# The first tile's last twelve products in both arms of a branch, and a row of conversions moved among the last expert's further tiles

## The chip, the cores and the metric

The kernel runs on one core of one Trainium2 chip. A time is the time of one execution in microseconds (us) as the device measures it; of several runs the median is given. The profile is of one execution, which has its own time.

## The reference

Sliding-window attention with a few sink positions is followed by a mixture of eight experts, and that by a gated layer (GLU). Of these the middle one matters here:

```python
expert_idx = np.argmax(x @ w_gate, axis=1)            # 1536 tokens, 8 experts
# token i takes the next free row of its expert, up to capacity = 384 rows
h = np.maximum(np.einsum('ecd,edf->ecf', disp, w1), 0.0)   # d = 512, f = 1024
y = np.einsum('ecf,efd->ecd', h, w2)
out[i] = gate_w[i] * y[expert_idx[i], pos[i]]
# GLU: sigmoid(x @ w_gate) * (x @ w_val) @ w_out, 1536 x 512 -> 1536 -> 512
```

How many tokens an expert gets is known only while the kernel runs.

## The kernel before, in words

All products are done at about fp32's precision: an operand is split into a high part (rounded to the matmul's type) and a low part (the rest), and a product is taken as high x high, low x high and high x low. `products` therefore lists twelve matmuls for a 128 x 512 x 512 product: four with the high activations and the high weights, four with the low activations, four with the low weights. ScalarE (ACT) makes a high part by a cast, VectorE (DVE) the low part by a subtraction that needs the cast's result.

`experts` runs over the experts e = 0 to 7. Each expert has up to three tiles of 128 rows. The first tile is computed always, the second and third under `If` on the expert's count (`more_tiles`, L837 and L839). In this run's data experts 0 and 7 have three tiles, 3 and 5 have two, and 1, 2, 4 and 6 have one. A tile goes through these steps:

- `turn_x` (L730 to L734): TensorE (PE) turns the rows, ACT casts `xh`, DVE subtracts `xl`.
- two times twelve products with the two halves of w1 into `u`, each followed by a relu on ACT (L763, `hr`); `turn_h` (L769 to L773) turns its result into `hh` and `hl`. The turns stand six products late, so that PE has work while ACT does the relu.
- twelve products with each half of w2; the second twelve need the second `hh` and `hl`. Then ACT copies the result to `yr` (L778), and `put_y` turns it (L787) and puts it into `yh` and `yl`, the input of the GLU (L789, L790).

For the first tile of an expert `put_y` stands in the next expert, behind twelve products. For the second and third tiles nothing stands between a tile's steps but what is shown here: a second tile starts with `turn_x` behind the branch.

All engines work off their own instructions in program order. Beside the tiles, ACT and DVE split the weights of the next expert (`split_next`, L132 and L133: 1024 columns each), ten halves ahead; the last three of an expert's splits stand ahead of the branch. The GLU's weights come as 64-bit floats and are converted: `whole` turns 512 columns by one ACT step (L150) and three DVE steps (L151, L153, L157), `convert` splits them (L164 on ACT, L165 on DVE). In the last expert `whole(0)` and `convert(0)` stand ahead of the branch, and seven further calls are the list `fills`; `beside()` in a tile takes the next one, and the arms for fewer tiles do what is left (`rest`).

PE, ACT and DVE each take the branch by themselves; an arm that is not taken is jumped over.

Of the kernel before, what the change touches and what calls it, by code (L numbers as in the profile page):

```python
# [9 lines left out]
F32 = mybir.dt.float32  # L10
# [10 lines left out]
P = 128  # L21
SUB = 1024
# [4 lines left out]
def kernel(  # L27
# [16 lines left out]
    nc = tc.nc  # L44
# [8 lines left out]
    N = B * S  # L53
# [644 lines left out]
    def experts(yh, yl):  # L698
        with ExitStack() as st:
# [27 lines left out]
            def turn_x(raw, more):  # L727
                t = ps_t.tile([P, KD, P], F32, tag="t", name="t")
                for k in range(KD):
                    nc.tensor.transpose(t[:, k], raw[:, k * P:(k + 1) * P], ident)  # L730
                h_ = ht.tile([P, KD, P], F32R, tag=f"xh{more}", name="xh")
                l_ = ht.tile([P, KD, P], F32R, tag=f"xl{more}", name="xl")
                nc.scalar.copy(out=h_, in_=t)  # L733
                nc.vector.tensor_sub(out=l_, in0=t, in1=h_.bitcast(F32))  # L734
                return h_, l_
# [7 lines left out]
            def weights(n):  # L743
                t = pair[n % NDBL].rearrange("p w (b k f) -> p w k b f", b=2, k=4)
                return t[:, 0], t[:, 1]
# [27 lines left out]
                nc.vector.tensor_sub(out=l_, in0=t, in1=h_.bitcast(F32))  # L773
                return h_, l_

            def raw_y(ps, more):
                t = hp.tile([P, 512], F32, tag=f"yr{more}", name="yr", bufs=1)
                nc.scalar.copy(out=t, in_=ps)  # L778
                return t

# [16 lines left out]
                nc.vector.tensor_copy(out=yh[:, d], in_=z)  # L797
                nc.gpsimd.tensor_copy(out=yl[:, d], in_=z)

            def more_tiles(e, fills):  # L800

                w1a, w1b, w2a, w2b = (weights(4 * e + x) for x in range(4))

                def one(j, todo):
                    def beside():
                        for f in todo[:1]:
                            f()
                        del todo[:1]

                    x = turn_x(xe[:, j - 1], 1)  # L810
                    u = bank(ps_u, 1)
                    go(products(u, x, w1a, True, True))
                    beside()
                    ra = relu(u)
                    u = bank(ps_u, 1)
                    b = products(u, x, w1b, True, True)
                    go(b[:6])
                    ha = turn_h(ra, 0)
                    beside()
                    go(b[6:])  # L820
                    rb = relu(u)
                    beside()
                    y = bank(ps_y, 1)
                    a = products(y, ha, w2a, True, False)
                    go(a[:6])
                    hb = turn_h(rb, 1)
                    beside()
                    go(a[6:])
                    go(products(y, hb, w2b, False, True))
                    return raw_y(y, 1)  # L830

                def rest(todo):
                    for f in todo:
                        f()

                n = 4 * (len(fills) + 1) // 8
                with tc.If(cnt_e[e] > P) as more:  # L837
                    put_y(e, 1, one(1, fills[:n]))
                    with tc.If(cnt_e[e] > 2 * P) as most:  # L839
                        put_y(e, 2, one(2, fills[n:]))  # L840
                    if fills:
                        with most.Else():
                            rest(fills[n:])
                if fills:
                    with more.Else():
                        rest(fills)

            V = nc.vector
            xs = {0: load_x(0), 1: load_x(1)}
# [5 lines left out]
            for e in range(E):  # L855
                w1a, w1b, w2a, w2b = (weights(4 * e + j) for j in range(4))
                m = 8 * e
                if e:
                    load_x_next(e + 2)
                    load_more(e)  # L860
                    split_next(m + 2, V)
                    split_next(m + 3, V)
                u = bank(ps_u, 0)
                go(products(u, x, w1a, True, True))
                ra = relu(u)
                if e:
                    put_y(e - 1, 0, yr)
                    split_next(m + 4, V)
                else:
                    cnt_x = counts([nc.sync.engine])  # L870
                    for j in range(1, E):
                        nc.sync.dma_start(
                            out=slots[j * ROWS:(j + 1) * ROWS, :][bass.ds(cnt_x[j], P), :], in_=zero)
                    load_more(e)
                    load_x_next(2)
                u = bank(ps_u, 0)
                b = products(u, x, w1b, True, True)
                go(b[:6])
                ha = turn_h(ra, 0)
                if e:  # L880
                    split_next(m + 5, V)
                go(b[6:])
                rb = relu(u)
                if e:
                    split_next(m + 6, V)
                if e + 1 < E:
                    x = turn_x(xs[e + 1], 0)
                y = bank(ps_y, 0)
                a = products(y, ha, w2a, True, False)
                go(a[:6])  # L890
                hb = turn_h(rb, 1)
                if e:
                    split_next(m + 7, V)
                go(a[6:])
                if e:
                    split_next(m + 8, V)
                    split_next(m + 9, V)
                elif e == 0:
                    cnt_e = counts([nc.tensor.engine, nc.scalar.engine, nc.vector.engine])
                go(products(y, hb, w2b, False, True))  # L900
                yr = raw_y(y, 0)
                if e == 0:
                    pi = order(hp)
                elif e < 7:
                    order_ids(pi, 2 * (e - 1), 2 * e)
                fills = []
                if e + 1 == E:
                    whole(0, 0, SUB)
                    convert(0)
                    load_glu(4, 0)  # L910
                    for q in range(1, 4):
                        fills += [partial(whole, q, h * 512, h * 512 + 512) for h in range(2)]
                        if q == 1:
                            fills.append(partial(convert, 1))
                more_tiles(e, fills)
            load_glu(5, 1)
            load_ids()
            put_y(E - 1, 0, yr)

            kept = nc.values_load(  # L920
                cnt_i[0:1, 2 * E:], engines=[nc.scalar.engine, nc.vector.engine], min_val=0, max_val=N,
                skip_runtime_bounds_check_because="a count of the tokens")
            z = zeros.unsqueeze(1).to_broadcast([P, KD, P])
            nc.scalar.copy(out=yh[:, :, bass.ds(kept, P)], in_=z)
            nc.vector.tensor_copy(out=yl[:, :, bass.ds(kept, P)], in_=z)
            for q in range(2, 4):
                convert(q)
                load_glu(q + 4, q)
# [270 lines left out]
```

## Time and profile before

| | us |
|---|---|
| median of 3 runs (lowest and highest) | 661.77 (659.67 to 663.36) |
| the profiled execution: its time | 662.41 |
| its span, first to last instruction | 660.7 |
| PE busy in the span | 613.9 |
| DVE, ACT busy | 359.7, 306.1 |
| experts, first product to the GLU's first | 147.61 to 363.26 |

The span is what the rows below are measured in; the time is 1.71 us longer. PE's clock has two levels, 2.4 GHz (granted clock 1.00) and 1.2 GHz (0.50); its mean over the span is 0.964.

### The profile page before, as it was taken

The numbers are of one execution on the slowest core, as the hardware profiler recorded it, in microseconds if no ns is written. First come the engines' busy times: TensorE is split into PE (matmuls) and PEld (weight loads), VectorE is DVE, ScalarE is ACT, GpSimd is POOL, SyncE is SP. The second block draws the span as 40 slices with busy tenths as digits, with TensorE's granted clock in tenths as the row PEclk, the third lists the DMA queues.
The fourth block names the chain that finished last, engine by engine and source line by source line (L and its number), as shares of the span: only waits on it lengthen the run. The fifth ranks groups of instructions, "written<-read, shape, count | busy, mean of one in ns | idle before, by whom it ended". The sixth has DMA issues, their size and how long they took to land.

```text
span 660.7 us, 9362 instructions
## 1 busy us (share of the span) xinstructions
PE 613.9 (93%) x3323; PEld 507.5 (77%) x3323; DVE 359.7 (54%) x871; ACT 306.1 (46%) x590; POOL 109.2 (17%) x163
## 2 busy tenths in 40 slices
PE   9899989989799899989697999999999997999995
PEld 5888888947577677767575888888888886889993
DVE  3465556534128655828754999981238811128911
ACT  4567757512238656838643655551225411125411
POOL 3155868472400000000000000000200000200002
PEclk9899969989999899999899899999999999799999
DMA  8987967142009963937712555551102520102101
GB/s 195 289 240 241 320 166 228 50 148 96 0 1 303 319 208 101 340 102 229 255 60 64 191 191 191 191 191 64 63 1 81 189 113 4 59 9 73 55 1 68
DMA packets 43638, 94.07 MB, mean 142 GB/s; under 512 B 5664, under 2 KB 24352, under 8 KB 39728
## 3 DMA queue, kind: packets, MB, share of 16 engines
q1 hardware_dynamic: 39872, 86.24, 40.5%
q0 software_dynamic: 2304, 6.09, 2.5%
q10 hardware_dynamic: 1392, 0.86, 0.5%
q8 instruction: 38, 0.62, 0.4%
q14 instruction: 32, 0.26, 0.1%
HBM read 82.63 MB, written 10.75 MB: 141 GB/s over the span
## 4 chain that ended last, share of the span: by engine, by line
issue 27%; PE 21%; ACT 2%; POOL 1%; DVE 1%; POOLq 0%; DVEq 0%; ACTq 0%
PE u L759 4%; PE g L168 4%; PE g L170 4%; PE g L169 4%; PE acc L170 2%; PE acc L168 2%; PE acc L169 2%; POOL out_dram L1024 1%; PE t L769 0%; DVE stage L153 0%; ACT pair L132 0%; ACT yr L778 0%; ACT hh L772 0%; PE t L787 0%; DVE stage L157 0%
## 5 line engine op out<-in xcount | busy, mean ns | idle before, releaser
L168 PE MATMUL g<-yh,pair 128*128 128x512 f32 (+1 forms) x288 | 110.4, 383 | 7.7 <-issue 4.6
L169 PE MATMUL g<-yl,pair 128*128 128x512 f32 (+1 forms) x288 | 110.0, 382 | 0.0
L170 PE MATMUL g<-yh,pair 128*128 128x512 f32 (+1 forms) x288 | 109.9, 382 | 0.0
L1024 POOL DMA_INDIRECT out_dram<-o,ids x11 | 10.8, 980 | 468.4 <-ACT o L1040 465.9
L759 PE MATMUL u<-pair,xh 128*128 128x512 f32 x224 | 64.4, 416 | 12.4 <-ACT xh L733 9.0
L992 DVE TENSOR_TENSOR g<-g,g 128x512 f32<-128x512 f32 (+1 forms) x36 | 23.4, 651 | 91.4 <-PE g L170 89.4
L993 ACT CAST gh<-g 128x512 fp32r<-128x512 f32 (+1 forms) x36 | 21.4, 594 | 110.6 <-DVE g L992 106.6
L133 DVE TENSOR_TENSOR pair<-stage,pair 128x1024 fp32r<-128x1024 f32 x54 | 64.2, 1220 | 11.7 <-ACT pair L132 11.3
L168 PEld LDWEIGHTS g<-yh,pair 128*128 128x128 f32 x288 | 55.2, 192 | 17.0 <-issue 5.0
L132 ACT CAST pair<-stage 128x1024 fp32r<-128x1024 f32 x64 | 65.3, 1050 | 3.0 <-PEq L837 1.5
L759 PE MATMUL u<-pair,hh 128*128 128x512 f32 x224 | 61.5, 400 | 2.7 <-ACT pair L132 1.8
L169 PEld LDWEIGHTS g<-yl,pair 128*128 128x128 f32 x288 | 55.3, 192 | 8.3
L759 PEld LDWEIGHTS u<-pair,xh 128*128 128x128 f32 x224 | 42.5, 197 | 24.6 <-ACT xh L733 10.6
L170 PEld LDWEIGHTS g<-yh,pair 128*128 128x128 f32 x288 | 55.2, 192 | 7.9
L296 ACT ACTIVATE pt<-sc,neg 128x260 f32<-128x260 f32 (+1 forms) x96 | 44.6, 491 | 33.6 <-DVE neg L285 33.5
L759 PEld LDWEIGHTS u<-pair,hh 128*128 128x128 f32 x224 | 40.7, 188 | 15.3 <-ACT pair L132 5.3
L991 ACT ACTIVATE g<-g 128x512 f32<-128x512 f32 (+1 forms) x36 | 20.5, 569 | 68.6 <-PE g L170 68.6
L170 PE MATMUL acc<-pair,gl 128*128 128x512 f32 x132 | 51.6, 391 | 0.0
L169 PE MATMUL acc<-pair,gh 128*128 128x512 f32 x132 | 51.5, 390 | 0.0
L168 PE MATMUL acc<-pair,gh 128*128 128x512 f32 x132 | 51.4, 390 | 0.0
L331 PE MATMUL pv<-v,pts 128*128 128x73 f32 x352 | 43.7, 278 | 0.0
L331 PEld LDWEIGHTS pv<-v,pts 128*128 128x128 f32 x352 | 43.0, 199 | 0.0
(157 smaller groups left out, 1031.2 us busy)
## 6 DMA issues: line engine op xcount, KB each, us to landing
stage<-in_we_dram SPq DMA_DIRECT2D x64, 512.0 KB
stage<-in_wd_dram SPq DMA_DIRECT2D x30, 1024.0 KB
vraw<-in_vr_dram SPq DMA_DIRECT2D x11, 288.0 KB
kraw<-in_kd_dram SPq DMA_DIRECT2D x22, 132.0 KB
qraw<-in_qd_dram SPq DMA_DIRECT2D x22, 128.0 KB
vt<-in_vt_dram SPq DMA_DIRECT2D x11, 256.0 KB
slots<-zero SPq DMA_DIRECT2D x1, 2048.0 KB
xs<-slots SPq DMA_DIRECT2D x8, 256.0 KB
```

The lines of the kernel that those rows point to most:

```text
L132: nc.scalar.copy(out=t[:, 0], in_=raw)
L133: eng.tensor_sub(out=t[:, 1], in0=raw, in1=t[:, 0].bitcast(F32))
L168: nc.tensor.matmul(ps, ah, bh, start=start, stop=False)
L169: nc.tensor.matmul(ps, ah, bl, start=False, stop=False)
L170: nc.tensor.matmul(ps, al, bh, start=False, stop=stop)
L296: nc.scalar.activation(out=pt_[i][:, h, :w], in_=scs_[n][j][:, :w], func=AF.Exp, scale=-1.0, bias=neg_[i][:, h:h + 1],)
L331: nc.tensor.matmul(pv_[n][:, h], pts_[n, h // 2][:, h % 2, j], vb[kb][:, 4 * a + h], start=(h == 0 and j == 0), stop=(h == 3 and j == len( ...
L759: nc.tensor.matmul(ps, a, b, start=start, stop=stop)
L991: nc.scalar.activation(out=g, in_=pss[0], func=AF.Sigmoid)
L992: nc.vector.tensor_tensor(out=g, in0=g, in1=pss[1], op=ALU.mult)
L993: nc.scalar.copy(out=gh[:, :w], in_=g)
L1024: nc.gpsimd.indirect_dma_start(out=out_v[j], out_offset=bass.IndirectOffsetOnAxis(ap=ids[:, j:j + 1], axis=0), in_=o, in_offset=None, boun ...
```

## The change

Three things are done. First, the last twelve products of the first tile no longer stand ahead of the branch. They are listed (`b`) and given to `more_tiles`. Where the expert has one tile, the Else arm runs them. Where it has more, the second tile runs four of them behind its `turn_x` and eight behind its last product, ahead of `put_y`; the first tile's result is copied (`raw_y(y, yr)`) after that `put_y`. So the first tile's second `hh` and `hl` are still read in the second tile, which gets buffers of its own (`turn_h(rb, 2)`). Second, in the last expert `whole(0)` and `convert(0)` become part of `fills`, now ten calls. The second tile takes five of them and the third five, by up to two at each `beside()`. Third, `load_glu(4, 0)` stands behind `more_tiles`, and the zeroing of 128 columns of `yh` and `yl` behind the last `put_y` (L920 to L925) is taken out.

```diff
-            def raw_y(ps, more):
-                t = hp.tile([P, 512], F32, tag=f"yr{more}", name="yr", bufs=1)
+            def raw_tile(more):
+                return hp.tile([P, 512], F32, tag=f"yr{more}", name="yr", bufs=1)
+
+            def raw_y(ps, t):
                 nc.scalar.copy(out=t, in_=ps)
                 return t
...
-            def more_tiles(e, fills):
+            def more_tiles(e, y, b, fills):
                 w1a, w1b, w2a, w2b = (weights(4 * e + x) for x in range(4))
-
-                def one(j, todo):
+                yr = raw_tile(0)
+
+                def one(j, todo, cover):
+                    todo = list(todo)
+                    per = -(-len(todo) // 4)
+
                     def beside():
-                        for f in todo[:1]:
+                        for f in todo[:per]:
                             f()
-                        del todo[:1]
+                        del todo[:per]
 
                     x = turn_x(xe[:, j - 1], 1)
+                    go(cover[:4])
                     u = bank(ps_u, 1)
                     go(products(u, x, w1a, True, True))
                     beside()
...
-                    hb = turn_h(rb, 1)
+                    hb = turn_h(rb, 2)
                     beside()
                     go(a[6:])
-                    go(products(y, hb, w2b, False, True))
-                    return raw_y(y, 1)
+                    go(products(yx, hb, w2b, False, True))
+                    r = raw_y(yx, raw_tile(1))
+                    go(cover[4:])
+                    put_y(e, j, r)
...
                 with tc.If(cnt_e[e] > P) as more:
-                    put_y(e, 1, one(1, fills[:n]))
+                    one(1, fills[:n], b)
+                    raw_y(y, yr)
                     with tc.If(cnt_e[e] > 2 * P) as most:
-                        put_y(e, 2, one(2, fills[n:]))
+                        one(2, fills[n:], [])
...
-                if fills:
-                    with more.Else():
-                        rest(fills)
+                with more.Else():
+                    go(b)
+                    raw_y(y, yr)
+                    rest(fills)
+                return yr
...
-                go(products(y, hb, w2b, False, True))
-                yr = raw_y(y, 0)
...
                 if e + 1 == E:
-                    whole(0, 0, SUB)
-                    convert(0)
-                    load_glu(4, 0)
-                    for q in range(1, 4):
+                    for q in range(4):
                         fills += [partial(whole, q, h * 512, h * 512 + 512) for h in range(2)]
-                        if q == 1:
-                            fills.append(partial(convert, 1))
-                more_tiles(e, fills)
+                        if q < 2:
+                            fills.append(partial(convert, q))
+                yr = more_tiles(e, y, products(y, hb, w2b, False, True), fills)
+            load_glu(4, 0)
             load_glu(5, 1)
             load_ids()
             put_y(E - 1, 0, yr)
-
-            kept = nc.values_load(
-                cnt_i[0:1, 2 * E:], engines=[nc.scalar.engine, nc.vector.engine], min_val=0, max_val=N,
-                skip_runtime_bounds_check_because="a count of the tokens")
-            z = zeros.unsqueeze(1).to_broadcast([P, KD, P])
-            nc.scalar.copy(out=yh[:, :, bass.ds(kept, P)], in_=z)
-            nc.vector.tensor_copy(out=yl[:, :, bass.ds(kept, P)], in_=z)
```

Lines of the changed kernel are numbered anew: the two branches are L848 and L851, the copy to `yr` is L780, the turn in `put_y` L789.

On PE, at the branch of expert 3 (the names are the written tile and what it is made of; `pair_84` holds the second half of w2, `pair_86` the first half of w1). Before:

```order
L759 MATMUL u<-pair_88,hh 128x512 x4
L759 MATMUL u<-pair_84,hh 128x512 x4
L759 MATMUL u<-pair_84,hl 128x512 x4
L759 MATMUL u<-pair_84,hh 128x512 x4
L837 COMPARE_AND_BRANCH
L730 MATMUL t<-ident,xe 128x128 x4
L759 MATMUL u<-pair_86,xh 128x512 x4
```

Now, at the same place:

```order
L759 MATMUL u<-pair_88,hh 128x512 x4
L848 COMPARE_AND_BRANCH
L730 MATMUL t<-ident,xe 128x128 x4
L759 MATMUL u<-pair_84,hh 128x512 x4
L759 MATMUL u<-pair_86,xh 128x512 x4
L759 MATMUL u<-pair_86,xl 128x512 x4
```

Twelve products stood between the last product of the first half of w2 and the second tile's turn; four now stand behind the turn, and the other eight behind the second tile's own last twelve.

On ACT, at the end of expert 3's second tile, where the third would begin. Before:

```order
L772 CAST hh<-t 128x512
L778 COPY yr<-u 128x512
L782 TENSOR_LOAD cnt_i
L789 ISA
L789 COPY yh<-t 128x4x128
L839 COMPARE_AND_BRANCH
L733 CAST xh<-t 128x512
```

Now:

```order
L772 CAST hh<-t 128x512
L780 COPY yr<-u 128x512
L784 TENSOR_LOAD cnt_i
L791 ISA
L791 COPY yh<-t 128x4x128
L780 COPY yr<-u 128x512
L851 COMPARE_AND_BRANCH
L733 CAST xh<-t 128x512
```

The first tile's copy, which stood ahead of the first branch, is now one more instruction of ACT between the second tile's `yh` and the third tile's `xh`.

On DVE, in the last expert's second tile, between its first `hl` and its second (`stage` holds the GLU's raw weights). Before:

```order
L773 TENSOR_TENSOR hl<-t,hh 128x512
L151 TENSOR_SCALAR stage_81<-stage_81 128x512
L153 SCALAR_TENSOR_TENSOR stage_81<-stage_81 128x512
L157 SCALAR_TENSOR_TENSOR stage_81<-stage_81 128x512
L165 TENSOR_TENSOR pair_86<-stage_81,pair_86 128x512 x2
L773 TENSOR_TENSOR hl<-t,hh 128x512
```

Now:

```order
L773 TENSOR_TENSOR hl<-t,hh 128x512
L165 TENSOR_TENSOR pair_86<-stage_80,pair_86 128x512 x2
L151 TENSOR_SCALAR stage_81<-stage_81 128x512
L153 SCALAR_TENSOR_TENSOR stage_81<-stage_81 128x512
L157 SCALAR_TENSOR_TENSOR stage_81<-stage_81 128x512
L151 TENSOR_SCALAR stage_81<-stage_81 128x512
L153 SCALAR_TENSOR_TENSOR stage_81<-stage_81 128x512
L157 SCALAR_TENSOR_TENSOR stage_81<-stage_81 128x512
L773 TENSOR_TENSOR hl<-t,hh 128x512
```

There is one `whole` more between the two. In the third tile it is three `whole` where it was two.

## Rows read from the trace of the kernel before

**Rows 1.** Who PE waited for, 145 to 375 us: total us, times, longest.

```profile
PE u L759 <- ACT xh L733: 9.0, 7, 4.5
PE t L787 <- ACT yr L778: 6.1, 6, 2.7
...
PE u L759 <- PEq L837: 2.1, 1, 2.1
```

**Rows 2.** Timeline of expert 7 at its branch: start, us, engine, line, instruction, [idle before].

```profile
320.69 1.20 PE L759 MATMUL u<-pair,hh 128*128 128x512 f32 x4 [0.22 <-ACT pair L132]
...
328.70 2.07 PE L759 MATMUL u<-pair,xh 128*128 128x512 f32 x4 [4.53 <-ACT xh L733]
```

**Rows 3.** Windows: us, busy (x instructions) of PE, PEld, DVE, ACT, POOL; PEclk, DMA.

```profile
328.70:333.20 4.50, 4.50 (x11) 3.53 (x12) 2.51 (x5) 0.52 (x1) 0.00 (x0) 0.50 0.65 233
...
179.60:183.00 3.40, 3.40 (x10) 2.63 (x9) 0.44 (x1) 0.00 (x0) 0.00 (x0) 0.50 0.00 0
...
224.00:227.40 3.40, 3.40 (x10) 2.62 (x9) 2.36 (x2) 1.56 (x2) 0.00 (x0) 0.50 0.98 358
```

**Rows 4.** Groups of instructions, 323.5 to 363 us: busy us, mean ns | idle before.

```profile
L153 DVE SCALAR_TENSOR_TENSOR stage<-stage 128x512 int32<-128x512 int32 x8 | 5.5, 693 | 3.0 <-ACT stage L150 2.4
L157 DVE SCALAR_TENSOR_TENSOR stage<-stage 128x512 int32<-128x512 int32 x8 | 5.5, 692 | 0.2
...
L165 DVE TENSOR_TENSOR pair<-stage,pair 128x512 fp32r<-128x512 f32 x4 | 2.7, 690 | 0.3
L164 ACT CAST pair<-stage 128x512 fp32r<-128x512 f32 x4 | 2.6, 670 | 2.1 <-DVE stage L157 2.1
L151 DVE TENSOR_SCALAR stage<-stage 128x512 int32<-128x512 int32 x6 | 2.5, 420 | 0.0
```

**Rows 5.** Timeline of expert 7's second tile (two rows) and third tile (the last).

```profile
337.11 0.60 ACT L763 ACTIVATE hr<-u 128x512 f32<-128x512 f32 x1 [0.24 <-PE u L759]
...
338.21 0.60 PE L769 MATMUL t<-ident,hr 128*128 128x128 f32 x4
...
356.24 1.19 PE L759 MATMUL u<-pair,hl 128*128 128x512 f32 x4 [0.27 <-DVE hl L773]
```

**Rows 6.** Timeline from the experts to the GLU.

```profile
362.59 0.62 ACT L924 CAST yh<-zeros 128x512 f32 x1 [0.76 <-DVE yl L790]
...
363.26 0.50 PE L168 MATMUL g<-yh,pair 128*128 128x512 f32 x1 [3.08 <-ACT yh L924]
...
363.60 0.39 PE L169 MATMUL g<-yl,pair 128*128 128x512 f32 x1
```

**Rows 7.** Timeline of expert 3 around its branch, and its second tile's end (last row).

```profile
234.66 2.95 ACT L132 CAST pair<-stage 128x1024 fp32r<-128x1024 f32 x3
235.77 1.19 PE L759 MATMUL u<-pair,hh 128*128 128x512 f32 x4 [0.23 <-ACT pair L132]
235.82 3.48 DVE L133 TENSOR_TENSOR pair<-stage,pair 128x1024 fp32r<-128x1024 f32 x3
...
238.62 0.60 PE L730 MATMUL t<-ident,xe 128*128 128x128 f32 x4
239.95 1.20 PE L759 MATMUL u<-pair,xh 128*128 128x512 f32 x4 [0.73 <-ACT xh L733]
...
252.76 0.66 PE L787 MATMUL t<-ident,yr 128*128 128x128 f32 x4 [0.68 <-ACT yr L778]
```

**Rows 8.** Timeline of expert 0: at its branch (two rows), and at its second tile's end.

```profile
159.23 0.17 DVE L684 TENSOR_TENSOR pi<-pk,pd 128x12 int32<-128x12 f32 x1
...
161.38 0.96 PE L759 MATMUL u<-pair,xh 128*128 128x512 f32 x3 [0.73 <-ACT xh L733]
...
177.37 0.66 PE L787 MATMUL t<-ident,yr 128*128 128x128 f32 x4 [2.66 <-ACT yr L778]
...
179.19 1.31 PE L759 MATMUL u<-pair,xh 128*128 128x512 f32 x3 [0.73 <-ACT xh L733]
```

**Rows 9.** The branch on PE's own queue: count, ns (least, median, most), first and last start.

```profile
L837 PEldq COMPARE_BRANCH  x8: 70/206/3646, 157.5 to 322.0; - x8
```

More of the change, by code (lines that the diff above doesn't have):

```diff
@@ L815, in one @@
                     u = bank(ps_u, 1)
-                    b = products(u, x, w1b, True, True)
-                    go(b[:6])
+                    c = products(u, x, w1b, True, True)
+                    go(c[:6])
                     ha = turn_h(ra, 0)
                     beside()
-                    go(b[6:])
+                    go(c[6:])
                     rb = relu(u)
                     beside()
-                    y = bank(ps_y, 1)
-                    a = products(y, ha, w2a, True, False)
+                    yx = bank(ps_y, 1)
+                    a = products(yx, ha, w2a, True, False)
                     go(a[:6])
-                    hb = turn_h(rb, 1)
+                    hb = turn_h(rb, 2)
                     beside()
                     go(a[6:])
-                    go(products(y, hb, w2b, False, True))
-                    return raw_y(y, 1)
+                    go(products(yx, hb, w2b, False, True))
+                    r = raw_y(yx, raw_tile(1))
+                    go(cover[4:])
+                    put_y(e, j, r)
                 def rest(todo):
```

## The prediction

> **What bounds the kernel now.** PE is busy in 613.9 of the span's 660.7 us (the table above), so the change can only give back what is left idle on PE between 147 and 363 us, and what PE loses there by running at half clock. I read four views for that. The waits of PE in that stretch come first [rows 1]: seven waits for `xh`, the first thing a tile's products need, 9.0 us in all with one of 4.5; and six for the copy to `yr`, 6.1 us. They are the two places at which the change puts products. The timeline then shows what kept ACT. In the last expert ACT and DVE convert a GLU weight ahead of the second tile's `xh`, and PE stands 4.53 us [rows 2]. In the others ACT is free, and `xh` costs the cast itself, 0.73 us [rows 7, 8]; the copy to `yr` 0.68 us [rows 7], except in expert 0, where it came late for a reason that I don't see (2.66 us [rows 8]). The windows show what comes on top: behind the long waits PE is busy throughout, but at a granted clock of 0.50 (1.2 GHz): 4.50 us in the last expert, 3.40 us in expert 0, and 3.40 us in expert 2, behind the one wait of 2.1 us for a branch [rows 1, 3]. Behind a wait of 0.73 us four products take 1.20 us and not 2.07 as behind that of 4.53 [rows 2, 7], so a short wait doesn't bring it. At 0.50 half of such a stretch is lost. Last, the hand-over to the GLU: its first product waits 3.08 us for the zeroing of `yh` [rows 6].
>
> **How I place the moved work.** Twelve products last 238.62 - 235.77 = 2.85 us with their start [rows 7], so 0.23 us each: four 0.9, eight 1.8. The moved products are the same ones, so what counts is when the second tile's products start, with 1.8 us added for the eight that are now behind it. Four turns are 238.62 to 239.95 less the wait of 0.73, 0.6 us [rows 7], or 0.5 where they follow other work.
>
> **The last expert, its branch.** The products ahead of the moved twelve end at 320.69 - 0.22 = 320.47 [rows 2]. Turn until 320.97, four products until 321.9. ACT has just ended the weight cast that released PE at 320.69, and the GLU's conversion no longer stands ahead, so `xh` (0.6 us) is there at 321.6: no wait. The tile's products start at 321.9, which with the eight owed is 323.7 against 328.70: 5.0 us. No long wait, so no half clock behind it: half of 4.50 us, 2.25 [rows 3].
>
> **The last expert, the conversions.** They don't vanish; each tile now takes more. One `whole` is 0.42 + 0.69 + 0.69 = 1.8 us of DVE, one `convert` 2 x 0.69 = 1.4 us of DVE and 2 x 0.67 of ACT [rows 4]. In the third tile before, two `whole` between the two `hl` already made PE wait 0.27 us for the second [rows 5]. Now three stand there: 1.8 more. In the second tile now, two `whole` and a `convert` stand there: 0.27 + 1.4. Its `convert` also stands ahead of the second relu on ACT. The relu waited 0.24 us for PE and ended at 337.71, 0.5 us ahead of its turn at 338.21 [rows 5]; two casts more are 1.34, so 1.34 - 0.24 - 0.5 = 0.6 us of waiting, by which PE itself is then later for `hl`, which leaves 1.05 there. New waits 0.6 + 1.05 + 1.8 = 3.45 us. That is the term that takes back most.
>
> **Second to third tile (experts 0 and 7).** The eight products cover the copy to `yr`: 0.68 us. But the first tile's copy now stands between `yh` and `xh` on ACT, about 0.5 us, so that wait is 1.2 and not 0.73. Net 0.2 in expert 7. So expert 7 gives 5.0 + 2.25 - 3.45 + 0.2 = 4.0 us.
>
> **The zeroing.** The GLU's second product needs the last `yl`, which was done just before the zeroing began at 362.59; it started at 363.60 [rows 6]. Without the zeroing it starts at 362.6: 1.0 us. The first product alone could start earlier, but the second stops it.
>
> **Expert 0.** No weights are split here. The moved products began at 160.06 - 2.75, about 157.3 (the row at 161.38, less its wait and the turn, gives 160.06). Turn until 157.8, four products until 158.7, `xh` long there. But `xl` follows on DVE only behind the token order, whose last instruction ends at 159.40 [rows 8]: ready at 160.1, 0.5 us late for the second group of four. So 158.7 + 0.5 + 1.8 = 161.0 against 161.38: 0.4 us. At the second tile's end the 2.66 us shrink by the 1.8 us of cover: 1.8. The copy on ACT costs 0.5. With 0.85 and 1.2 us in place of 2.66 I take the half clock as gone: half of 3.40, 1.7 [rows 3]. Sum 0.4 + 1.8 - 0.5 + 1.7 = 3.4 us.
>
> **Experts 3 and 5 lose.** Here three weight splits stand ahead of `xh` and `xl`, and so far the twelve products covered them. Expert 3: the products ahead end at 235.77 - 0.23 = 235.54, the turn at 236.0, four products at 236.95; ACT's casts end at 234.66 + 2.95 = 237.61, so `xh` at 238.2: a wait of 1.25 us in place of 0.73. Four products until 239.1; DVE's three subtractions end at 235.82 + 3.48 = 239.30 [rows 7], `xl` at 240.0: 0.9 us more. Before, the second group of four stood at 239.95 + 0.95 = 240.9. So 0.9 early, 1.8 owed, 0.68 given back at `yr`: 0.2 us lost, in each of the two.
>
> **What costs nothing.** Experts 1, 2, 4 and 6 run the same twelve products behind the jump and not ahead of it, with the same queue in front. `load_glu(4, 0)` starts later, but its weights are converted only in the GLU, which starts at 363.26 [rows 6]; what hides it are the last expert's own tiles, and if it came late ACT and DVE would be late with a GLU step, not PE at once. The third pair of `hh` and `hl` takes room, not time.
>
> **The sum.** 4.0 + 1.0 + 3.4 - 0.4 = 8.0 us. Against it stand new idle stretches of PE that the profile has no exact match for: 2.1 us in expert 7's third tile, 1.25 and 0.9 close together in experts 3 and 5, 0.85 and 1.2 in expert 0. Do they bring the half clock? The nearest rows: behind 2.1 us it came [rows 1, 3], behind a single wait of 0.73 it did not [rows 2, 7]. So between nothing and 4 x 1.7 = 6.8 us. The 2.1 is nearest to a stretch that brought it; I count one, 1.7. That leaves 6.3 us: 662.41 - 6.3 = 656.1 on the profiled execution's own time. The median of the runs is 0.64 below that execution, so **655.5 us**.
>
> **Rival 1: the half clock at all four places.** The gain is 8.0 - 6.8 = 1.2 us, 660.5 us, which cannot be told from no change: I call 0.5% (3.3 us) the bound of that. For it: each place has about 2 us idle in all, near the 2.1 that brought it. Against it: in three of them turns or products stand between. Chance 0.15.
>
> **Rival 2: it gives more.** Expert 0's late copy had no visible cause; if it doesn't recur, the remaining 0.85 us go as well, and no half clock comes back anywhere: 8.0 + 0.85, so 662.41 - 8.85 - 0.64 = 652.9 us. For it: the six waits for that copy sum to 6.1, so without this one they are 0.7 each [rows 1]. Against: a cause that I can't see is one that I can't call removed. Chance 0.15.
>
> **Rival 3: slower, by jumps that wait for code.** The profile shows eight branches on PE's queue, median 206 ns, but one of 3646 [rows 9]. That one (expert 2, a far jump over two tiles; DMA is busy 0.98 of the time right behind it [rows 3]) left PE idle 2.1 us [rows 1] and brought the half clock, 1.7: 3.8 us. The change makes every far jump longer by the twelve products and gives experts 0, 3, 5 and 7 a jump over the Else arm. If three more jumps do as expert 2's did, it is 11.4 us: 655.5 + 11.4 = 666.9, slower than before; from two of them on (7.6 us) the gain is gone. Against it: PE waited for this branch once in eight [rows 1], though experts 1, 4 and 6 jump as far, and the new jumps are short, over twelve products. Chance 0.06.
> The Trainium skill (Runtime: NRT & Kernel Launch, Instruction fetch mechanics) speaks for this rival: a taken branch whose target lies outside the pages held makes the engine fetch that page by DMA before it goes on. By that rule alone the far jumps of experts 1, 4 and 6 would each cost about what expert 2's did, before as now, and the short ones nothing; the trace agrees in one of four.
>
> **How the numbers follow.** My sum has 0.62, rivals 1, 2 and 3 have 0.15, 0.15 and 0.06, the rest 0.02. My sum's own spread, with none to two half clocks, is 653.8 to 657.2. Faster by over 0.5%, that is below 658.5, are my sum less 0.04 (if two terms come out short), rival 2 and half the rest: 0.74. Within 0.5% are rival 1 and that 0.04: 0.19. Slower are rival 3 and half the rest: 0.07. The range 651 to 660.5 takes in rivals 2 and 1, each at its end, and leaves out rival 3.
>
> **What would show it.** Right: the wait for `xh` of 4.5 us gone and the waits for `yr` gone but for the third tiles' own and one in expert 0; new waits for `hl` in expert 7, about 1 and 2 us; for `xh` and `xl` in experts 3 and 5, 1.2 and 0.9. The GLU's first product waits for `put_y`'s `yh`. Wrong: waits of PE for its queue of over 2 us at other branches than expert 2's, half clock in experts 3 and 5, a wait of the GLU for its first converted weights.

## The result, and the profile after

The changed kernel takes 651.81 us, the median of four runs (649.8 to 655.24), the kernel before beside it 661.26 (four runs, 659.67 to 663.36). The ratio is 0.987, 95% interval 0.9825 to 0.9914. Predicted were 655.5 us and a range of 651.0 to 660.5.

The profiled execution is the slowest of the four: 655.24 us, span 653.4. Against the 662.41 us of the one before it is 7.2 us; the sum had 6.3. Who PE waited for, 145 to 375 us (total, times, longest), to be read beside [rows 1]:

```profile
PE u L759 <- ACT xh L733: 6.5, 5, 2.1
PE u L759 <- DVE hl L773: 3.2, 2, 2.1
PE t L789 <- issue: 2.1, 1, 2.1
PE g L168 <- ACT yh L791: 1.7, 1, 1.7
...
PE u L759 <- DVE xl L734: 1.5, 3, 0.6
PE t L789 <- ACT yr L780: 1.5, 2, 0.7
PE u L759 <- PEq L851: 0.9, 2, 0.4
```

The wait of 4.5 us for `xh` is gone, as forecast. So is one that I expected to stay: the 2.1 us for the branch of expert 2 (L837 before, L848 now). The timeline of PE gives the places:

```profile
147.42 1.19 PE L759 MATMUL u<-pair,xh 128*128 128x512 f32 x4 [0.80 <-ACT xh L733]
...
175.05 0.66 PE L789 MATMUL t<-ident,yr 128*128 128x128 f32 x4 [2.07 <-issue]
178.24 2.08 PE L759 MATMUL u<-pair,xh 128*128 128x512 f32 x4 [2.07 <-ACT xh L733]
...
204.37 1.15 PE L759 MATMUL u<-pair,hh 128*128 128x512 f32 x4 [0.32 <-ACT pair L132]
217.81 1.17 PE L759 MATMUL u<-pair,hh 128*128 128x512 f32 x4 [0.40 <-ACT pair L132]
233.52 1.19 PE L759 MATMUL u<-pair,xh 128*128 128x512 f32 x4 [1.18 <-ACT xh L733]
235.33 0.50 PE L759 MATMUL u<-pair,xl 128*128 128x512 f32 x1 [0.62 <-DVE xl L734]
...
260.01 1.17 PE L759 MATMUL u<-pair,hh 128*128 128x512 f32 x4 [0.32 <-ACT pair L132]
302.18 1.17 PE L759 MATMUL u<-pair,hh 128*128 128x512 f32 x4 [0.32 <-ACT pair L132]
316.55 1.09 PE L759 MATMUL u<-pair,xh 128*128 128x512 f32 x4
328.26 1.20 PE L759 MATMUL u<-pair,hl 128*128 128x512 f32 x4 [1.07 <-DVE hl L773]
334.29 1.20 PE L759 MATMUL u<-pair,xh 128*128 128x512 f32 x4 [1.22 <-ACT xh L733]
346.75 2.08 PE L759 MATMUL u<-pair,hl 128*128 128x512 f32 x4 [2.13 <-DVE hl L773]
351.11 1.09 PE L789 MATMUL t<-ident,yr 128*128 128x128 f32 x8 [0.73 <-ACT yr L780]
353.91 0.80 PE L168 MATMUL g<-yh,pair 128*128 128x512 f32 x1 [1.70 <-ACT yh L791]
```

In expert 7 the second tile starts without a wait at 316.55; its `hl` waits 1.07 us, the third tile's 2.13. Experts 3 and 5 (one shown) wait 1.18 and 0.62 us. Expert 0's copy to `yr` is late as before (2.07 us), and a second wait of 2.07 us follows.

The first row, the four of 204.37 to 302.18 (the first of the last twelve products of experts 1, 2, 4 and 6) and the GLU's first product cut the experts into five stretches. The same four rows of the kernel before:

```profile
204.70 1.20 PE L759 MATMUL u<-pair,hh 128*128 128x512 f32 x4 [0.23 <-ACT pair L132]
218.45 1.20 PE L759 MATMUL u<-pair,hh 128*128 128x512 f32 x4 [0.23 <-ACT pair L132]
264.49 1.20 PE L759 MATMUL u<-pair,hh 128*128 128x512 f32 x4 [0.23 <-ACT pair L132]
306.95 1.20 PE L759 MATMUL u<-pair,hh 128*128 128x512 f32 x4 [0.22 <-ACT pair L132]
```

Gain by stretch, as the sum had it and as these rows give it (us):

| | expert 0 | 1 | 2 and 3 | 4 and 5 | 6 and 7 | all |
|---|---|---|---|---|---|---|
| predicted | 3.4 | 0 | -0.2 | -0.2 | 4.0 + 1.0 - 1.7 = 3.3 | 6.3 |
| measured | 0.14 | 0.31 | 3.84 | 0.29 | 4.58 | 9.16 |

The rest of the span is 1.9 us longer than before. It lies in the GLU, and a_again, the same kernel, has 1.6 us less there; so most of it is not the change's.

### The profile page after: what moved, and what is told of

Its sections match the earlier page's. It is cut to its first block, busy times and chain, and to the rows that moved or that the text cites. A ratio compares the mean times of both kernels' runs of the same rounds, so it can differ in the third digit from the quotient of the medians.

```text
span 653.4 us, 9352 instructions
## 1 busy us (share of the span) xinstructions
PE 611.8 (94%) x3323; PEld 508.6 (78%) x3323; DVE 359.3 (55%) x870; ACT 304.7 (47%) x589; POOL 109.2 (17%) x163
## 4 chain that ended last, share of the span: by engine, by line
issue 45%; PE 6%; DMA 1%; DVE 1%; ACT 1%; POOL 1%; POOLq 0%; SPq 0%; DVEq 0%; ACTq 0%
PE u L759 5%; DMA ids<-idsd 1%; POOL out_dram L1027 1%; DMA out_dram<-o,ids 0%; PE t L769 0%; ACT pair L132 0%; DVE stage L153 0%; ACT hh L772 0%; POOLq L1196 0%; DVE hl L773 0%; PE t L730 0%; PE t L789 0%; DVE pair L165 0%; ACT stage L150 0%; DVE stage L157 0%
## 5 line engine op out<-in xcount | busy, mean ns | idle before, releaser
L759 PE MATMUL u<-pair,xh 128*128 128x512 f32 x224 | 62.3, 406 | 7.3 <-ACT xh L733 6.5
L168 PE MATMUL acc<-pair,gh 128*128 128x512 f32 x132 | 51.4, 390 | 0.0
```

The lines of the kernel that those rows point to most:

```text
L168: nc.tensor.matmul(ps, ah, bh, start=start, stop=False)
L759: nc.tensor.matmul(ps, a, b, start=start, stop=stop)
```

## The experiments

Single times scatter by 3 us and more, so the verdicts below come from the stretches of each kernel's profile, and the times stand beside them. A time is followed by the lowest and highest run, and by its ratio to the kernel before with the 95% interval. Stretches in us, differences of the same six rows as above:

| | expert 0 | 1 | 2 and 3 | 4 and 5 | 6 and 7 | all |
|---|---|---|---|---|---|---|
| before | 57.09 | 13.75 | 46.04 | 42.46 | 56.31 | 215.65 |
| before_again | 57.05 | 13.75 | 44.92 | 42.52 | 56.55 | 214.79 |
| changed | 56.95 | 13.44 | 42.20 | 42.17 | 51.73 | 206.49 |
| a_again | 57.04 | 13.47 | 42.11 | 42.30 | 50.41 | 205.33 |
| b_nocover | 58.46 | 13.42 | 42.13 | 42.15 | 52.06 | 208.22 |
| c_ahead | 56.94 | 13.42 | 42.15 | 42.12 | 53.73 | 208.36 |
| d_zero | 57.04 | 13.43 | 42.17 | 42.19 | 53.13 | 207.96 |
| e_spread | 58.11 | 13.42 | 42.12 | 43.76 | 45.97 | 203.38 |
| f_scatter | 51.58 | 13.57 | 57.87 | 42.09 | 50.21 | 215.32 |
| g_splits | 59.33 | 13.42 | 40.72 | 40.69 | 51.81 | 205.97 |
| h_all | 58.90 | 13.43 | 40.25 | 40.23 | 45.56 | 198.37 |
| i_all_glu | 51.35 | 13.41 | 40.21 | 40.18 | 45.49 | 190.64 |
| j_glu | 51.61 | 13.43 | 42.05 | 42.13 | 51.45 | 200.67 |

**a_again: the changed kernel, unaltered.**

> The changed kernel once more, for a second profile. Its profiled execution took 655.24 us, its three others 649.8 to 651.8. Theory 1: expert 0's late copy to yr (2.07 us of PE's time in the profiled execution, then 2.07 us for xh and 1.7 us of half clock) is missing in the quick executions; a profile of one at about 651 us then shows waits of 0.7 us at both places. Rival: the copy is as late as before in a quick execution, and the 3.4 us come from another stage (the attention or the GLU). Expected median 651.8 us.

Measured: 654.46 us, median of six (651.76 to 656.45), 0.9895 (0.9839 to 0.9951). Its profiled execution took 652.41 us. PE's timeline:

```profile
175.06 0.66 PE L789 MATMUL t<-ident,yr 128*128 128x128 f32 x4 [2.13 <-issue]
...
347.08 1.19 PE L759 MATMUL u<-pair,hl 128*128 128x512 f32 x4 [2.14 <-DVE hl L773]
352.72 0.51 PE L168 MATMUL g<-yh,pair 128*128 128x512 f32 x1 [1.70 <-ACT yh L791]
```

The late copy is there in a quicker execution too, so theory 1 falls. What differs is the clock behind the same wait. The changed kernel's first profile and this one, windows behind `hl` (us, busy of PE, PEld, DVE, ACT, POOL, PEclk, DMA share):

```profile
346.70:350.10 3.40, 3.35 (x8) 2.48 (x8) 0.00 (x0) 0.00 (x0) 0.00 (x0) 0.50 0.00 0
```

```profile
347.00:350.40 3.40, 2.59 (x12) 1.90 (x13) 0.03 (x1) 0.59 (x1) 0.00 (x0) 1.00 0.00 0
```

Half clock behind 2.13 us in the one, full clock behind 2.14 in the other: 1.2 us in the last stretch. From the GLU's first product to the end of the span it is 299.49 against 297.88 us: in the first profile PE also starts the GLU at half clock for longer. These two make up the 2.8 us between the two spans.

**b_nocover: the twelve products at the head of both arms.**

```diff
-                    one(1, fills[:n], b)
+                    go(b)
                     raw_y(y, yr)
+                    one(1, fills[:n], [])
```

> The last twelve products of the first tile stand at the head of both arms, and cover neither the second tile's xh nor its yr; the conversions stay moved and the zeroing stays out. Theory 1, read from the waits of the changed kernel: the cover is worth little. In expert 7 it comes to 0.73 + 0.68 - 0.5 = 0.9 us lost without it; experts 3 and 5 gain 2.22 - 1.41 = 0.8 us each; expert 0 about the same. So 651.8 - 0.7, about 651 us. Rival: the cover is the main gain (the 5.0 us at expert 7's branch), and without it the time is 655 us or more. In both, expert 2's branch should not stop PE again if it is the place of the branch, ahead of the twelve products, that hides the jump; if a stop of over 2 us is back, it is chance or the cover.

Measured: 650.84 us (649.52 to 658.89), 0.9856 (0.979 to 0.9921). By the stretches the cover is worth nothing in experts 3 and 5, 1.5 us in expert 0 (both have the half clock there for 6.8 us), and in expert 7 52.06 - 50.41 = 1.65 us against the profile that, like this one, has no half clock behind `hl`. Theory 1's 0.7 us quicker is wrong in sign, though the median came where it had it: without the cover the experts take 208.22 us and not 205.3 to 206.5, as experts 3 and 5 give nothing back for it. Nor is it the rival's main gain. Expert 2's branch stops PE no more, cover or not.

**c_ahead: the conversions ahead of the branch again.**

```diff
+                    whole(0, 0, SUB)
+                    convert(0)
-                    for q in range(4):
+                    for q in range(1, 4):
...
-                        if q < 2:
+                        if q == 1:
```

> The cover stays; the last expert's first whole and first convert stand ahead of the branch again (seven fills, one at each beside). Theory 1: the moved conversions are the main gain. PE waits about 6.4 us for expert 7's xh, the half clock of 2.2 us is back behind it, and the waits for hl shrink from 1.07 and 2.13 us to none and 0.3 with their half clock of 1.7: 6.4 + 2.2 - 1.2 - 1.9 - 1.7 = 3.8 us slower, 655.6 us. Rival (the cover is the gain): within 1 us of the changed kernel, 652 us.

Measured: 655.26 us (649.97 to 660.07), 0.9894 (0.9825 to 0.9964).

```profile
321.61 2.08 PE L759 MATMUL u<-pair,xh 128*128 128x512 f32 x4 [4.32 <-ACT xh L733]
```

The wait for `xh` and its half clock are back, 4.3 us instead of 6.4 forecast; the `hl` waits are gone but for 0.27 us. The last stretch takes 2.0 us more than in the changed kernel, 3.3 more than in a_again. Moving the conversions thus gives more than the cover, though less than theory 1 had.

**d_zero: the zeroing back.** It follows `put_y(E - 1, 0, yr)`:

```diff
+            kept = nc.values_load(
+                cnt_i[0:1, 2 * E:], engines=[nc.scalar.engine, nc.vector.engine], min_val=0, max_val=N,
...
+            z = zeros.unsqueeze(1).to_broadcast([P, KD, P])
+            nc.scalar.copy(out=yh[:, :, bass.ds(kept, P)], in_=z)
+            nc.vector.tensor_copy(out=yl[:, :, bass.ds(kept, P)], in_=z)
```

> The zeroing of 128 columns of yh and yl is put back behind the last put_y. Theory 1: the GLU's second product starts 1.0 us later, as the prediction's term has it: 652.8 us. Rival: PE's half clock at the GLU's start is set by that wait too, so a longer wait costs more, 2 us: 653.8 us; or the zeroing hides behind other work, 651.8 us.

Measured: 653.36 us (648.04 to 659.22), 0.9867 (0.9805 to 0.9928). The GLU's first product:

```profile
359.38 0.80 PE L168 MATMUL g<-yh,pair 128*128 128x512 f32 x1 [3.08 <-ACT yh L933]
```

3.08 us of waiting instead of 1.70, so 1.4; the last stretch is longer by the same 1.4. (This is the slowest of the six runs, 659.22 us; 4.0 us of that lie ahead of the first expert, outside the stretches.) The term of 1.0 went by the second product, which gains 1.1. Theory 1, slightly undersized.

**before_again: the kernel before, unaltered.**

> The kernel before once more, for a second profile. Theory 1: the place of its branch, behind twelve products that PE's queue holds, makes expert 2's jump visible, so PE waits about 2 us for it again, with the half clock behind it (46.0 us from expert 2's to expert 4's last twelve products; the changed kernel and its variants took 42.1 to 42.2 in five profiles). Rival: the wait was a chance of one execution; then this stretch takes 42.3 to 42.6 us, and 3.8 us of the measured gain are not the change's.

Measured: 657.73 us, one run. PE's timeline, and the branch on PE's queue (ns: least, median, most):

```profile
220.36 1.15 PE L759 MATMUL u<-pair,xh 128*128 128x512 f32 x4 [2.56 <-PEq L837]
```

```profile
L837 PEldq COMPARE_BRANCH  x8: 70/206/4086, 153.9 to 317.3; - x8
```

The stop recurs, 2.56 us, this time without half clock. In eleven profiles with the branch ahead of the twelve products it never does, with the cover or without, with the conversions and the zeroing moved or not. So it is no chance; what makes the difference is read from the traces in the next section.

**e_spread: the conversions dealt out anew.**

```diff
-                    per = -(-len(todo) // 4)
+                    take = [2, 1, 0, 2]
...
-                        for f in todo[:per]:
-                            f()
-                        del todo[:per]
+                        for _ in range(take.pop(0)):
+                            if todo:
+                                todo.pop(0)()
```

> The last expert's conversions are dealt out as 2, 1, 0 and 2 calls over a tile's four places, instead of 2, 2, 1 and 0. Theory: the waits for hl come from the five DVE conversions between the two hl; with one convert or one whole there both waits (1.1 and 2.1 us) are gone, and with them the half clock that stands behind the longer one in some executions (1.2 us). The experts then take 203.2 us where the changed kernel took 206.5 and 205.3. Rival: the work put behind the second hl delays the next tile's xh or put_y's yl, and the wait only moves: 205 us or more.

Measured: 645.91 us (643.19 to 651.27), 0.9738 (0.9688 to 0.9788). PE no longer waits for `hl` at all, the next wait in expert 7 is this:

```profile
334.89 1.20 PE L759 MATMUL u<-pair,xh 128*128 128x512 f32 x4 [1.22 <-ACT xh L733]
```

It is the same 1.22 us as in the changed kernel, so in expert 7 nothing moved. The last stretch is 5.8 us shorter (4.4 against a_again). This execution has a half clock that none other shows, in expert 5 behind the usual 1.18 and 0.61 us (1.6 us in its stretch). In expert 0 the copy to `yr` came later still: PE waited 4.30 us for it, as it did in g_splits (4.21) and h_all (4.16). That is why expert 0 takes 58 to 59 us in these three.

**f_scatter: the token order's 12 scatters beside expert 2.**

```diff
-                    pi = order(hp)
-                elif e < 7:
-                    order_ids(pi, 2 * (e - 1), 2 * e)
+                    pi0 = order(hp)
+                elif e == 1:
+                    pi = const.tile([P, NTILE], I32, name="pi2")
+                    nc.vector.tensor_copy(out=pi, in_=pi0)
+                else:
+                    order_ids(pi, 2 * (e - 2), 2 * (e - 1))
```

> The token order is copied once on DVE in expert 1, and the 12 scatters on POOL wait for that copy, so that they run beside expert 2 instead of expert 0. Theory: they are what makes expert 0's copy to yr late, since its lateness ends with the last scatter in every profile (174.4 to 174.8 us); without them the wait of 2.1 us is gone, the one for xh behind it falls from 2.1 to 1.2, and the half clock behind goes: expert 0 takes 3 to 4 us less (53 to 54 us where it took 57.0), and expert 2 may show such a late copy instead. Rival: the copy is late for another reason in expert 0, and its waits stay as they are.

Measured: 661.74 us (656.86 to 663.63), 0.9998 (0.9958 to 1.0037). PE's timeline:

```profile
173.11 1.20 PE L759 MATMUL u<-pair,xh 128*128 128x512 f32 x4 [1.22 <-ACT xh L733]
...
227.46 2.07 PE L759 MATMUL u<-pair,hh 128*128 128x512 f32 x4 [7.02 <-ACT pair L132]
239.44 1.09 PE L730 MATMUL t<-ident,xe 128*128 128x128 f32 x4 [7.01 <-DVE pair L133]
```

In expert 0 the late copy and its half clock are gone, 5.4 us, which is more than the 3 to 4 of the theory. But experts 2 and 3 lose 15.7: weights come late, and ACT's casts wait for their DMA, once for 4.38 us:

```profile
226.36 1.04 ACT L132 CAST pair<-stage 128x1024 fp32r<-128x1024 f32 x1 [4.38 <-DMA stage<-in_we_dram]
```

The same 21 us of the span in this kernel and in the changed one, with the scatters on POOL and without:

```profile
201.00:222.00 21.00, 18.97 (x96) 15.21 (x95) 15.25 (x16) 15.74 (x21) 15.57 (x12) 1.00 1.01 199
```

```profile
201.00:222.00 21.00, 20.29 (x98) 16.19 (x97) 18.60 (x19) 17.40 (x24) 0.00 (x0) 1.00 0.93 317
```

The last column is GB/s: the DMA engines are as busy (1.01 and 0.93), and move 199 instead of 317. The changed kernel reaches the same code 7 us later, and from 208 to 229 us it moves 342. In the trace a 4 KB packet of the weights takes 337 ns here and 190 in the changed kernel, in the mean; the median is 159 in both, so some packets are held up for long. That I had not foreseen.

**g_splits: the last two weight splits inside the second tile.**

```diff
-                    split_next(m + 8, V)
-                    split_next(m + 9, V)
...
                     hb = turn_h(rb, 2)
+                    rest(ahead)
...
                 with more.Else():
+                    rest(ahead)
                     go(b)
...
-                yr = more_tiles(e, y, products(y, hb, w2b, False, True), fills)
+                late = (m + 8, m + 9) if 0 < e < E - 1 else ()
+                yr = more_tiles(e, y, products(y, hb, w2b, False, True), fills, [partial(split_w, i, V) for i in late])
+                for i in late:
+                    load_w(i + 8)
```

> The last two weight splits of an expert stand in the second tile, behind its second hl, or ahead of the twelve products in the Else arm, instead of ahead of the branch. Theory: they are what makes xh and xl late in experts 3 and 5 (1.2 and 0.6 us); without them ahead the cover hides xh wholly, and each of the two experts takes 1.5 us less: 40.7 us where it took 42.2. Rival: the splits then stand ahead of the copy to yr or of put_y, or the next expert's first products wait for them, and the gain is lost there.

Measured: 650.06 us (643.47 to 651.04), 0.9783 (0.9715 to 0.985). Both experts give the 1.5 us (40.72 and 40.69), although the next expert then waits a little for ACT at the join, where the arms of the branch meet again:

```profile
249.25 1.20 PE L759 MATMUL u<-pair,xh 128*128 128x512 f32 x4 [1.21 <-ACTq L852]
```

That was 0.4 in the changed kernel. Its expert 0 had the later copy, and the half clock for longer (59.33).

**h_all: spread and late splits together, and the copy ahead of `put_y`'s `yh`.**

```diff
                     go(cover[4:])
+                    if cover:
+                        raw_y(y, yr)
                     put_y(e, j, r)
```

> The spread conversions and the late splits together, and the first tile's copy to yr ahead of put_y's yh on ACT instead of behind it. Theory: the gains lie at different places and add up: expert 7 takes 46.0 us from expert 6's last twelve products to the GLU as with the spread alone, experts 3 and 5 take 40.7 us as with the late splits alone, and the copy's new place gives 0.5 us more in each expert with more than one tile: experts 199 us, time 641 us. Rival: the copy ahead of yh delays yh and so the GLU or the third tile's turn, and the sum is no better than 201 us.

Measured: 641.9 us (637.04 to 644.11), 0.9693 (0.9644 to 0.9743): the fastest of all, faster than both kernels. Experts 198.37 us; the gains add up, and the copy gives 0.4 to 0.5 us at each place: the third tile's `xh` waits 0.78 us instead of 1.22, the join too.

```profile
247.12 1.21 PE L759 MATMUL u<-pair,xh 128*128 128x512 f32 x4 [0.78 <-ACTq L853]
328.00 1.19 PE L759 MATMUL u<-pair,xh 128*128 128x512 f32 x4 [0.78 <-ACT xh L733]
```

**i_all_glu and j_glu: the scatters in the GLU**, with h_all and with the changed kernel.

```diff
-                    pi = order(hp)
-                elif e < 7:
-                    order_ids(pi, 2 * (e - 1), 2 * e)
+                    held_pi.append(order(hp))
...
-            load_ids()
...
+                    if t == 2:
+                        pi = const.tile([P, NTILE], I32, name="pi2")
+                        nc.vector.tensor_copy(out=pi, in_=held_pi[0])
+                        order_ids(pi, 0, NTILE)
+                    if t == 7:
+                        load_ids()
                     g = up(n, r, w)
```

> The same, and the 12 scatters of the token order stand in the GLU's third step, the load of the ids in its eighth. Theory: the scatters made expert 0's copy late (51.6 us without them there, 57.0 with them), and beside expert 2 they held back the weight loads (two waits of 7 us); the GLU's loads have more time, so nothing comes back there: experts 194 us, time 636 us. Rival: beside the GLU they make its weights or its first products late, by some of the 5.4 us or by more, as they did beside expert 2 (14 us).

> The changed kernel with only the scatters moved to the GLU. Theory: expert 0 takes 51.6 us instead of 57.0, nothing else changes: 5.4 us less than the changed kernel's 651.8 to 654.5 us, 646 to 649 us. Rival: the GLU gives the gain back, 652 us or more.

Measured: i_all_glu 643.47 us (638.8 to 645.87), 0.9731 (0.9689 to 0.9773); j_glu 653.39 (647.87 to 659.66), 0.9868 (0.9809 to 0.9927). Neither is clearly faster than the kernel that it was made from (641.9; 651.81 and 654.46). Expert 0 takes 51.4 and 51.6 us, as forecast. From the GLU's first product to the end it is 302.0 us against h_all's 296.4, and 304.7 against 299.5 and 297.9. So i_all_glu gives back 5.6 of the 7.6 us that expert 0 wins against h_all, and j_glu 5.2 to 6.8 of 5.4, part of it by a longer half clock at the GLU's start: mostly as the rival said. PE's waits in j_glu, 375 to 420 us, a place where the changed kernel has none:

```profile
PE acc L168 <- ACT gh L995: 4.7, 2, 2.8
```

## Why the prediction was right, and where it was not

The median is 3.7 us below the forecast and within the range (a_again's six runs of the same kernel: 1.0 below), but two steps failed, with opposite signs: expert 0 gave 3.3 us less than the sum had, experts 1 to 5 gave 4.8 more. That the two partly cancel is luck.

**The last expert: right, with some sizes off.** `xh`: no wait. `hl`: 1.05 and 2.1 us were forecast, 1.07 and 2.13 came; the third tile's `xh` 1.2, came 1.22; the relu 0.6, came 0.16. The 1.05 had been worked out with a relu of 0.6, so that 1.07 meets it is in part luck: together the two are 1.23 us, not 1.65. The half clock behind the third tile's `hl`, 1.7 in the sum, came in one of the two profiles and cost 1.2. The zeroing: 1.0 forecast, 1.4 by d_zero. c_ahead and b_nocover show that the two halves, moved conversions and cover, give about 3.3 us (the half clock behind the wait included) and 1.65. e_spread shows that the 3.45 us which the sum took off for conversions were the price of how they were dealt out, not of having them in the tiles.

**Experts 3 and 5: right.** Waits of 1.25 and 0.9 forecast, 1.18 and 0.62 measured, which together eat the cover; b_nocover puts the net at nothing, the sum at -0.2.

**Expert 0: the step that failed** is "At the second tile's end the 2.66 us shrink by the 1.8 us of cover". I took the lateness as a length that products can cover. It is a date, set by the scatters. In the changed kernel the last scatter on POOL and the copy on ACT start at

```profile
173.65 0.98 POOL L689 DMA_INDIRECT idsd<-ids,pi  x1 [0.30 <-issue]
```

```profile
174.41 0.59 ACT L780 COPY yr<-u 128x512 f32<-128x512 f32 x1 [6.75 <-remote]
```

though the products that it copies end at 171.2 (their last four start at 170.10). In ten profiles with the scatters there, the copy starts 0.8 us (four of them) or 2.9 to 3.1 us (six, both of before among them) after the last scatter does, whenever the products ended: in e_spread, g_splits and h_all they ended as early as in the changed kernel, and the copy took the later date. Products that end earlier wait longer; f_scatter and j_glu, without the scatters there, win 5.4 us. So `yr` and `xh` together still cost 4.1 us (3.4 before), and "I take the half clock as gone" failed with it. It held for 6.8 us where [rows 3] have 3.40, and that ate what the cover gave:

```profile
176.00:182.80 6.80, 4.73 (x13) 3.64 (x12) 1.39 (x2) 1.56 (x3) 0.00 (x0) 0.50 0.00 0
```

3.4 us were forecast, 0.14 measured.

**Experts 1, 2, 4 and 6: the other step that failed** is "the same twelve products behind the jump and not ahead of it, with the same queue in front". The jump now starts earlier. In the changed kernel:

```profile
L848 PEldq COMPARE_BRANCH  x8: 70/202/2377, 155.3 to 313.1; - x8
```

The longest is expert 2's, 215.3 to 217.6 us, and PE has work until 217.4 and then waits for a weight split till 217.81 anyway. Before, the longest was 3.65 us [rows 9], began at 219.8, and PE ran dry at 221.5:

```profile
L837 PEldq COMPARE_BRANCH  x2: 347/1996/3646, 206.0 to 219.8; - x2
```

```profile
220.40 1.07 PE L759 MATMUL u<-pair,hh 128*128 128x512 f32 x4
223.59 1.71 PE L759 MATMUL u<-pair,xh 128*128 128x512 f32 x4 [2.12 <-PEq L837]
```

So 2.1 us and the half clock, 3.8 in all, are won without the jump having gone, and before_again shows that the stop was no chance. Two things changed. The work that PE still had when the jump began is 2.15 us instead of 1.70. And the jump is shorter: 3.65 and 4.09 us in the two profiles of before, 1.2 to 2.5 in the eleven others. Its length goes with a packet of the trace: in all thirteen profiles it ends 1.25 to 1.36 us after a 16 KB packet of instructions has ended. Before, that packet starts 1.26 and 1.70 us after the jump does, in the eleven others between 1.1 us ahead of it and 0.1 behind. A jump of 3.65 us would still have stopped PE, by an estimated 3.65 - 2.15 = 1.5 us, so the queue alone does not explain the gain. Why the packet comes earlier is not shown: the new order and the new layout of the code came together in every run.

The other single-tile experts win 0.3 us each: before, the next expert's first four products started 1.22 us after the last four of this one (206.66 and 207.88 us), now 0.90 (206.26 and 207.16). At that branch PE's queue had a wait for a semaphore (four times 51 ns), which is gone; that fits, but was not tried alone.

**Rival 1** (half clock at all four places) did not come: expert 0 had it, expert 7's third tile in one of two profiles, experts 3 and 5 not; **rival 2**'s time nearly did (652.9), by another mechanism: the late copy recurred. **Rival 3** did not come: no jump of the experts stops PE in the changed kernel. The Trainium skill (Runtime: NRT & Kernel Launch, Instruction fetch mechanics) has a taken branch out of the held pages wait for a page that comes by DMA. The trace agrees for expert 2, whose jump goes with one 16 KB instruction packet at 215.34 us. The jumps of experts 1, 4 and 6 go without such a packet and take 0.31 to 0.33 us; whether their targets were held is not shown. What PE sees of a jump is what outlasts the work in its queue. A branch of the GLU, which the change leaves as it was, shows it: L1109 (L1106 before) takes two jumps one behind the other, and when the second begins, at 550.56 us in the changed kernel, PE has run dry (550.51); it goes on at 555.62, just behind the jump's end at 555.56. PE stands 4.5 to 5.3 us there in all thirteen profiles. PE's waits in the changed kernel, 340 to 660 us:

```profile
PE g L168 <- issue: 5.1, 1, 5.1
```

**Open.** Why scatters on POOL make ACT see PE's end late is not shown; only that expert 0's lateness goes when they go. Why expert 2's instruction packet comes earlier is not shown either. Nor is it shown why the clock falls behind a wait in one execution and not in the next.

## What to carry to other kernels

Work that covers a wait helps if the wait has a length; where it ends at a date that something else sets, find that first. For a branch, compare how long its jump lasts with the work that the engine still has when the jump begins: 3.65 us against 1.70 stopped PE here, 2.38 against 2.15 and a wait of 0.3 for a weight split, which stood there anyway, did not. Before paying for conversions moved among other steps, count per gap what the follower's operand must wait behind: two calls more or less at one place were worth 4 to 6 us here.

## What I had not expected of the hardware

- Twelve scatters of 128 small rows on POOL cost about 5 us beside quiet DMA (expert 0, DMA busy 0.02), 5 to 7 in the GLU, and 15.7 beside the weight loads, where the DMA engines stayed as busy and moved 199 GB/s instead of 317.
- The same wait brought the half clock in one execution and not in another: 2.13 and 2.14 us for `hl`; 1.18 and 0.61 us in expert 5, in one of seven profiles that have these waits; expert 2's stop, 2.12 us with it and 2.56 without. A forecast can give such a stretch a chance, not a yes or no.
